# A spectral filter and a gated feed-forward on one core: weight columns in two loads, table points in parts, four more zero matmuls, and a tie of GpSimd copies to a scaling

## The chip, the core and the metric

The kernel runs on one core of a Trainium2 chip. Its instructions are issued by five engines: PE (TensorE, matmuls; PEld is its load of stationary operands), ACT (ScalarE), DVE (VectorE), POOL (GpSimd) and SP (SyncE, which here only issues DMAs; POOL issues DMAs too). The metric is the time of one execution on the device in microseconds, as the median of several runs. "0.3%" means 0.3% of that median.

## The reference

The input x has 2048 rows (S) of 576 numbers (D). A layer norm, a global filter in the frequency domain, a residual; then a second layer norm, a gated feed-forward of width 4608 and a second residual. All arrays are bf16.

```python
def _A_ref(x, w_r, w_i):                      # w_r, w_i: 2048 x 289
    X = jnp.fft.rfft2(x.astype(jnp.float32), axes=(-2, -1))
    X = X * (w_r + 1j * w_i)
    return jnp.fft.irfft2(X, s=(S, D), axes=(-2, -1)).astype(jnp.bfloat16)

def _B_ref(x, w_gate, w_up, w_down):
    return (_gelu(x @ w_gate) * (x @ w_up)) @ w_down

h = x + _A_ref(_layernorm(x), A_w_r, A_w_i)
h2 = h + _B_ref(_layernorm(h), B_w_gate, B_w_up, B_w_down)
```

## The kernel before

**How the work is laid out.** Row s = 16 p + c stands in partition p and tile c, so XO holds 16 tiles of 128 x 576. The transform over S is made as a 128-point step (over the partitions) and a 16-point step (over the tiles), the one over D as a product with cosine and sine tables. All of it is matmuls with tables that the kernel loads from DRAM.

**The order is written out by hand** in three strings of tokens, one token for each step, and `LOADS` hangs weight loads on tokens. Each engine executes its own instructions in the order in which they are emitted; `Prog` (`op`, `dma`, `emit`) turns the read and write keys of each operation into semaphore waits. Between two operations on PE no wait is made, except where the code asks for one (`after`); a DMA counts as done when its semaphore has its full count.

- `SEQ1` is the front. `B`/`b`/`S`/`Q` gather the statistics of a tile, `v`, `q`, `c` make the reciprocal deviation of a group of tiles (GROUPS: 2, 2, 3, 3, 3, 3 tiles), `x` (`ln1_scale`, L517) scales the 128-point table ATB into ATS with it, on DVE (`x0D`, `x1D`, `x5D`) or POOL (`x2P`, `x3P`, `x4P`), `n` and `t` copy parts of x on POOL, `M` (`a_mm`, L540) is the 128-point step of a group, `E`/`F` (`a_ev`) evacuate its banks into U. `k` (`idle_mm`, L533) issues matmuls of a zero tile into the bank that the next `M` uses first: `k14`, `k104`, `k202` are 14, 4 and 2 of them, for groups 0, 1 and 2.
- `SEQF` is the middle, 16 groups g of frequencies in the order `GORD` (1 to 15, then 0, which is group number 15 in the string). `D`/`d` (`st_D`, L630, matmuls at L640) is the product with FT over D and its evacuation CUS; `B` (`st_B`, L654) is the 16-point step with the table BT; `T` (`st_T`, L665, on DVE at L673) multiplies by the spectral weights WS; `V`/`v` (`st_V`, L675) and `R`/`r` (`st_R`, L690) are the inverse 16-point step with the table VT, the first for 256 columns, the second for the remaining 32 of four groups at once; `r` moves its result into VR with small DMAs on SP and POOL. BT and VT have one part for groups 1 to 15 and others for group 0 (g = 0, the last one done); for `R` there is a reordered copy of each.
- `SEQ` is the end of the filter: `I`/`i` (`i_mm`, L822; matmuls at L830, which read V and, in the last of three steps, VR) and `N`/`o` (L840) are the inverse steps over D and S, `a` (`x_add`) adds the residual, `s`, `q`, `c`, `n` make the second norm, `u`/`U` (`turn_mm`) transpose a tile and `e` (`turn_ev`) evacuates it into HT0. `G0` and `G1` (`gu_first`, L954) are gate and up products of the first two feed-forward blocks (m = 0 and 1), for the first 256 rows and the next 256.

After that comes the feed-forward over four blocks of 512 rows: for each of 36 blocks f of 128 columns `gu_part` (L924, matmuls at L939), Gelu on ACT (L947), the product on DVE (L948), and then `down_pass` (L1039). In the first block, the second half of the filter's rows is done in between (`deferred`).

**Loads.** `LORD` gives the order of x and ATB on SP; behind it come, in this order on SP: FT, BT, the first half of the spectral weights (`w_up`, `w_down` for both planes), VT, the second half, the zero group (`w_zero`). `dup_w` then makes the duplicates of WS in the other 64 partitions: for the first groups two copies by POOL (L730) and two by DVE (L728), for the others DMAs issued by POOL, which wait for the weights. `last` is the last of these DMAs; `tab_load` (at `r0`) makes SP wait for it and then loads DT, IT and IDT. `tab2_load` (at `.i7`) loads DP and ITD.

**The first feed-forward weights** (slot 0: 576 rows of gate and of up, columns 0 to 1152, blocks f = 0 to 8) are loaded in ten DMAs by `wg0_part`, each behind a `hold()`: SP waits until PE has finished everything emitted for it so far. Only the tenth writes the keys of the slot, and all ten count on one semaphore, so that every matmul of f = 0 to 8 waits for all ten. Slots 1 and 2 follow behind G0, where SP and POOL both hold.

**Where things lie.** HT0 shares its place with FT, BT and VT, so HT0 waits until these have been read.

Of the kernel before, what the change touches and what calls it, by code (L numbers as in the profile page):

```python
# [15 lines left out]
NT = 16  # L16
# [6 lines left out]
GROUPS = ((0, 2), (2, 4), (4, 7), (7, 10), (10, 13), (13, 16))  # L23
SEQ1 = """B0 b0 S3 B2 Q3 n0 B1 b1 b2 n1 t0 m3P t2 v0 v1 n2 t1 q0 c0 k14 x0D q1 M0 E0A S4 m4P c1 x1D n3 E2A k104 b5 t3 b7 Q4 E1A M1 E7A B5 B6 E8A b6 B7 v2 q2 B11 E5A B8 c2 x2P E3A E9A b8 b9 B9 v3 E6A n4 B12 Q13 E4A k202 M2 b10 q3 c3 b11 S13 x3P E11A B10 t4 b12 v4 E10A B14 m13P E14A M3 q4 c4 x4P E12A E13A t5 b14 E15A b15 B15 v5 E16A E18D E17A q5 M4 E20A E19A E23A c5 x5D n5 E24A F24D F23D E21A M5 E25A E26D E22A E28D E27A E29D F25A F29D F26A F27A F28A F22A""".split()
LORD = "x0-2 x2-4 a0-4 x4-8 a4-8 x8-12 x12-16 a8-16".split()
# [4 lines left out]
DENG, BENG = ['act', 'dve', 'act', 'act', 'act', 'act', 'act', 'act', 'dve', 'act', 'act', 'act', 'act', 'act', 'act', 'act'], ['act', 'dve', 'act', 'act', 'act', 'act', 'act', 'dve', 'act', 'act', 'act', 'act', 'act', 'act', 'act', 'act']  # L30
LOADS = {"r0": "t", "v12": "0", "v15": "1", ".I0": "2", ".i1": "3", ".N0": "4", ".i3": "5", ".o1": "6", ".N3": "7", ".o3": "8 9", ".i7": "d"}
RENG = ['dve', 'act', 'act', 'act', 'act']
# [14 lines left out]
def build_tables():  # L47
# [106 lines left out]
    assert np.allclose(VN[0, 0], VN[0, 1])  # L154
    T["VTAB"] = np.stack([VN[0, 0], VN[1, 0], VN[1, 1]] + [v.reshape(128, 4, 16, 4).transpose(0, 1, 3, 2).reshape(128, 256) for v in (VN[0, 0], VN[1, 0], VN[1, 1])], 1).reshape(128, -1)

# [175 lines left out]
def _build(nc, A_x, A_w_r, A_w_i, B_w_gate, B_w_up, B_w_down, out):  # L332
# [90 lines left out]
    def bank(b, p0=0, p1=128, c0=0, c1=512):  # L423
        return PS[p0:p1, b * 512 + c0:b * 512 + c1]
# [21 lines left out]
    P.dma(SP, FT[:, :, :].rearrange("p a b -> p (a b)"), dram["FTAB"][:, :], "ft", w=["FT"])  # L446
    P.dma(SP, BT[:, :, :, :].rearrange("p a b c -> p (a b c)"), dram["BTAB"][:, :], "bt", w=["BT"])

# [20 lines left out]
    for pl in (1, 0):  # L469
        w_up(pl, 0)  # L470
        w_down(pl, 0)
    P.dma(SP, VT[:, :, :, :].rearrange("p a b c -> p (a b c)"), dram["VTAB"][:, :], "vt", w=["VT"])
    for pl in (1, 0):
        w_up(pl, 1)
        w_down(pl, 1, (0, 1, 2, 3) if pl else (0, 1))
    for pl in (1, 0):
        w_zero(pl)
    GORD = list(range(1, NG)) + [0]
    wkeys = [[("W", hf, pl, h) for pl in range(2) for h in range(6 if hf < 2 else 2)] for hf in range(3)]
# [175 lines left out]
    def st_B(i, eng=ACT):  # L655
        sl, s3, sp_ = i % NY, i % 3, 1 if GORD[i] == 0 else 0
        b0 = FB["B", i]
        for m in range(2):
            for h in range(2):
                P.op(PE, lambda t, m=m, h=h: t.matmul(bank(b0 + h, 0, 128, 0, KW), BT[64 * h:64 * h + 64, sp_, m, :], CUS[64 * h:64 * h + 64, s3, m, :], start=(m == 0), stop=(m == 1)),  # L660
                     r=[("CU", s3), "BT"], w=[("PS", b0 + h)])
        ev(eng, YS[:, sl, :, :], banks(b0, 2, KW), [("PS", b0), ("PS", b0 + 1)], [("Y", sl)])
# [13 lines left out]
    def st_V(i, second, engs):  # L676
        g, z, b0 = GORD[i], i % NZ, FB["V", i]

        def mm(h, o, ct, first, last, after):
            c, t_ = ct  # L680
            return P.op(PE, lambda t: t.matmul(bank(b0 + o, 0, 128, 128 * c, 128 * c + 128), TP[64 * h:64 * h + 64, z, o, t_, c:256:2], VT[64 * h:64 * h + 64, 0 if g else 1 + o, t_, :],  # L681
                                               start=first, stop=last), r=[("T", z), "VT"], w=[("PS", b0 + o)], after=after)

        halves(("V", i), second, [[(c, t_) for c in range(2) for t_ in range(2)]] * 2, mm)
        if not second:
            return
        v5 = V[:, :, :, :, g, :, :].rearrange("p c t n j e -> p j (c t n) e")
        n = 2 // len(engs)
        for a, e in enumerate(engs):
            ev(e, v5[:, n * a:n * a + n], banks(b0 + a, n, 256).rearrange("p a (c e) -> p a c e", e=4), [("PS", b0 + a + k) for k in range(n)], [("V", g, a + k) for k in range(n)])  # L690

    def st_R(q, second):
# [3 lines left out]
        def mm(h, o, pt, first, last, after):  # L696
            part, t_ = pt
            return P.op(PE, lambda t: t.matmul(bank(b0 + o, 0, 128, 128 * part, 128 * part + 128), TR[64 * h:64 * h + 64, q % 2, o, t_, :], VT[64 * h:64 * h + 64, 4 + o if part else 3, t_, :], start=first, stop=last),  # L698
                        r=[("TR", q % 2, j) for j in range(4)] + ["VT"], w=[("PS", b0 + o)], after=after)

# [18 lines left out]
    def dup_w(k, jp, pl=slice(0, 2), eng=None):  # L719
        a, b = 64 * jp, 64 - 64 * jp  # L720
        n = ("Wd", k, jp, pl.start)
        for g0, g1 in (((1, 6),), ((6, 9),), ((9, 13),), ((13, 16), (0, 1)))[k]:
            dst, src = (WS[q:q + 64, jp, pl, g0:g1, :].rearrange("p a g k -> p a (g k)")[:, :, 1:] for q in (b, a))
            r = [x for x in (wkeys[1] if g0 > 8 else wkeys[0] if g0 else wkeys[0] + wkeys[2]) if pl.start <= x[2] < pl.stop]
            if eng is None:
                op = P.dma(POOL, dst, src, f"wd{k}{jp}", r=r, w=[(*n, g0)])
            elif eng == DVE:
                P.op(DVE, lambda v: v.tensor_copy(dst, src), r=r, w=[(*n, g0)])  # L728
            else:
                P.op(POOL, lambda v: v.tensor_scalar(dst, src, 1.0, 1.0, op0=ALU.mult, op1=ALU.mult), r=r, w=[(*n, g0)])  # L730
        return op if eng is None else None
# [32 lines left out]

    def wg0_part(k):
        hold()
        src = (B_w_gate, B_w_up)[k % 2]
        if k < 8:
            P.dma(SP, WG3[:, 0, 4 * (k % 2) + k // 2, :], src[(0, 128, 320, 448)[k // 2]:(128, 256, 448, 576)[k // 2], 0:1152], "wg00")
        else:  # L770
            P.dma(SP, WG3[64 * (k % 2):64 * (k % 2) + 64, 0, 8, :], src[256:320, 0:1152], "wg00", w=[("WG", 0, i) for i in range(4)] if k == 9 else [])

    def loads(w):
        for v in LOADS.get(w, "").split():
            (tab_load if v == "t" else tab2_load if v == "d" else lambda: wg0_part(int(v)))()

# [18 lines left out]
    P.alias(sum(wkeys, []) + sum(dup, []), [("WG", j, k) for j in (1, 2) for k in range(4)])  # L795
    P.alias(["FT", "BT", "VT"], [("HT", 0, i, k) for i in range(4) for k in range(5)])

# [128 lines left out]
    def gu_part(m, second, c0=0, c1=512):  # L926
# [5 lines left out]
        for j in range(n):  # L932
            for half in range(2):
# [6 lines left out]
                    bank(b, 0, 128, c0, c1), wg_tile(slot)[h0:h0 + 64, wt, 128 * (f % 9):128 * (f % 9) + 128], HT[h0:h0 + 64, kt, c0:c1], start=s, stop=e),  # L940
                    r=[("HT", tb % 2, i, k) for i in range(c0 // 128, c1 // 128) for k in range(5)] + [("WG", slot, i) for i in range(4)],
                    w=[("PS", b)], after=aft)
# [182 lines left out]
```

## Time and profile before

| what | value |
|---|---|
| time, median of 3 runs (lowest to highest) | 488.34 us (487.86 to 489.21) |
| the profiled execution | 487.7 us, span 485.9 us |
| PE busy, 23.84 to 43.67 us | 19.77 of 19.83 us |
| PE busy, 43.67 to 57.22 us | 11.55 of 13.55 us |
| gate/up matmuls (L939), us busy | 233.3 with WG, 53.4 with WGX |
| down matmuls (L1039), us busy | 132.9 |
| the ten loads of slot 0, from issue to landing | 3.2 to 5.0 us, median 3.8 |
| DMA engines, 44 to 56 us | 3.16 MB, 263 GB/s |

A profile is one execution, seen by the hardware profiler. Its span runs from the first to the last instruction; the time around it is longer. "Busy" is the time in which an engine works; rows of instructions give start, duration, engine, source line, operation, output and inputs, shape and count, and in square brackets the idle time just before and what ended it. Pieces of the chain of waits give start, duration and what. Rows of loads give target, source, issuing queue, count, size of each and the median of the microseconds from issue to landing. "SPq" and "POOLq" are issues of DMAs; the share of the DMA engines is the mean busy share of 16 engines and can show a little over 1.

### The profile page before, as it was taken

How to read it: one execution, taken by the hardware profiler on the slowest of the kernel's cores; microseconds unless marked ns; L12 is line 12 of the kernel's file. 1: busy time of each engine (PE TensorE's matmuls, PEld its weight loads, DVE VectorE, ACT ScalarE, POOL GpSimd, SP SyncE). 2: the span in 40 equal slices, each digit the busy share in tenths (PEclk: the TensorE clock that was granted, in tenths of full speed). 3: DMA queues.
4: the chain of work that ended last, by engine and by line, in shares of the span. 5: the costliest groups of instructions: out<-in, count | busy, mean ns of one | idle time of the engine just before them, and what ended most of it. 6: DMA issues, size and time to landing. Idle time of an engine off the chain costs nothing.

```text
span 485.9 us, 12883 instructions
## 1 busy us (share of the span) xinstructions
PE 476.7 (98%) x5872; PEld 279.4 (57%) x5872; DVE 182.9 (38%) x366; ACT 146.6 (30%) x295; POOL 52.8 (11%) x88
## 2 busy tenths in 40 slices
PE   7899899999999999999999999999999999999998
PEld 3777665544477744444577644444777444444774
DVE  7898756566501133333200233333101233333011
ACT  6998664443400023322200023322100133223000
POOL 6873317010120000000000000000000000000000
PEclk9999999999999999999999999999999999999999
DMA  8965598941440001100000011000000000000000
GB/s 287 210 161 177 175 306 285 377 110 24 131 143 26 27 15 20 23 0 1 1 15 15 26 21 23 14 2 1 3 13 26 14 1 0 1 1 1 3 26 26
DMA packets 26966, 33.19 MB, mean 68 GB/s; under 512 B 12560, under 2 KB 19104, under 8 KB 26912
## 3 DMA queue, kind: packets, MB, share of 16 engines
q1 hardware_dynamic: 23248, 19.87, 14.7%
q0 software_dynamic: 3664, 12.50, 8.0%
q8 instruction: 46, 0.75, 0.7%
q14 instruction: 8, 0.07, 0.0%
HBM read 26.21 MB, written 2.36 MB: 59 GB/s over the span
## 4 chain that ended last, share of the span: by engine, by line
PE 93%; DMA 1%; DVE 0%; issue 0%; SPq 0%; DVEq 0%
PE PS L939 58%; PE PS L1039 27%; PE PS L1051 2%; PE PS L640 2%; PE PS L681 2%; DMA WG<-in_B_w_up_dram 1%; PE PS L830 1%; PE PS L660 1%; PE PS L989 1%; PE PS L847 1%; PE PS L1006 0%; PE PS L698 0%; DVE CUS L606 0%; DVE V L606 0%; SPq L242 0%
## 5 line engine op out<-in xcount | busy, mean ns | idle before, releaser
L939 PE MATMUL PS<-HT,WG 64*128 64x512 bf16 (+1 forms) x2142 | 233.3, 372 | 1.2 <-DMA WG<-in_B_w_up_dram 1.2
L939 PEld LDWEIGHTS PS<-HT,WG 64*128 64x128 bf16 x2142 | 105.2, 94 | 116.1 <-DMA WG<-in_B_w_up_dram 1.3
L947 ACT ACTIVATE GL<-PS 128x512 bf16<-128x512 f32 x144 | 85.7, 596 | 282.9 <-PE PS L939 282.9
L948 DVE TENSOR_TENSOR AT<-GL,PS 128x512 bf16<-128x512 bf16 x144 | 98.8, 687 | 167.1 <-ACT GL L947 167.1
L1039 PE MATMUL PS<-WD,AT 64*128 64x288 bf16 x2160 | 132.9, 283 | 0.0
L1039 PEld LDWEIGHTS PS<-WD,AT 64*128 64x128 bf16 x2160 | 103.3, 94 | 29.8
L1026 DVE TENSOR_TENSOR OS<-PS,XO 128x288 bf16<-128x288 f32 (+2 forms) x32 | 13.3, 453 | 125.5 <-PE PS L1039 118.0
L939 PE MATMUL PS<-HT,WGX 64*128 64x512 bf16 x486 | 53.4, 376 | 0.0
L939 PEld LDWEIGHTS PS<-HT,WGX 64*128 64x128 bf16 x486 | 23.2, 94 | 29.2
L856 ACT ACTIVATE OS<-XO,NM 128x576 bf16<-128x576 bf16 x15 | 11.6, 774 | 11.4 <-DVE XO L1010 11.4
L640 PE MATMUL PS<-FT,U 64*128 64x288 bf16 x160 | 13.5, 284 | 0.3 <-DVE CUS L606 0.3
L673 DVE TENSOR_TENSOR TP<-YS,WS 128x1024 bf16<-128x1024 bf16 x16 | 11.0, 688 | 0.5 <-DMA WS<-WS 0.5
L551 PE MATMUL PS<-ATS,XO 128*128 128x128 bf16 x96 | 8.2, 219 | 3.0 <-POOL ATS L520 2.1
L494 DVE BATCH_NORM_STATS2 ST<-XO 128x6 f32<-128x288 bf16 x26 | 9.9, 441 | 2.1 <-DMA XO<-in_A_x_dram 2.0
L562 ACT ACTIVATE U<-PS 128x384 bf16<-128x384 f32 (+2 forms) x31 | 10.4, 419 | 1.1 <-PE PS L551 0.9
L681 PE MATMUL PS<-VT,TP 64*128 64x128 bf16 x256 | 10.0, 217 | 0.0
L242 POOL DMA_DIRECT2D WG<-in_B_w_gate_dram x9 | 6.1, 678 | 35.1 <-DMA WG<-in_B_w_gate_dram 30.6
L551 PEld LDWEIGHTS PS<-ATS,XO 128*128 128x128 bf16 x96 | 6.9, 98 | 4.4 <-POOL ATS L520 2.9
L242 POOL DMA_DIRECT2D WD<-in_B_w_down_dram x9 | 6.7, 755 | 24.4 <-PE PS L1006 24.4
L606 ACT ACTIVATE CUS<-PS 128x576 bf16<-128x576 f32 x14 | 9.0, 653 | 0.8 <-PE PS L640 0.7
L1051 PE MATMUL PS<-WD,AT 128*128 128x448 bf16 (+1 forms) x72 | 9.0, 286 | 0.0
L606 ACT ACTIVATE YS<-PS 128x576 bf16<-128x576 f32 x14 | 8.8, 653 | 0.2
(88 smaller groups left out, 229.5 us busy)
## 6 DMA issues: line engine op xcount, KB each, us to landing
WD<-in_B_w_down_dram POOLq DMA_DIRECT2D x9, 576.0 KB, 10.6
WG<-in_B_w_up_dram SPq DMA_DIRECT2D x6, 576.0 KB, 6.8
WG<-in_B_w_gate_dram POOLq DMA_DIRECT2D x6, 576.0 KB, 5.8
out_dram<-OS SPq DMA_DIRECT2D x30, 72.0 KB, 1.7
XO<-in_A_x_dram SPq DMA_DIRECT2D x3, 576.0 KB, 7.5
WG<-in_B_w_gate_dram SPq DMA_DIRECT2D x4, 288.0 KB, 3.8
WG<-in_B_w_up_dram SPq DMA_DIRECT2D x4, 288.0 KB, 3.6
WGX<-in_B_w_up_dram SPq DMA_DIRECT2D x2, 576.0 KB, 4.6
```

The source lines that it names most:

```text
L242: fn = lambda e: e.dma_start(out_ap, in_ap)
L551: P.op(PE, lambda t, b=b, lhs=lhs, p0=p0, p1=p1, s=s, e=e, o=o, c=c: t.matmul(bank(b, p0, p1, o, o + 128), lhs, ATS[:, c, :], start=s, sto ...
L606: fn = (lambda v: v.tensor_copy(dst, src)) if eng == DVE else (lambda a: a.activation(dst, src, ACTF.Copy))
L640: return P.op(PE, lambda t: t.matmul(bank(b0 + o, 0, 128, 0, 2 * HK), U[64 * h:64 * h + 64, us, 2 * i:2 * i + 2, :, :], FT[64 * h:64 * h + ...
L681: return P.op(PE, lambda t: t.matmul(bank(b0 + o, 0, 128, 128 * c, 128 * c + 128), TP[64 * h:64 * h + 64, z, o, t_, c:256:2], VT[64 * h:64 ...
L856: P.op(ACT, lambda a, c=c, out=out: a.activation(out, XO[:, c, 0:D], ACTF.Square, bias=NM[:, c:c + 1], accum_out=SB2[:, 1, c:c + 1]), r=[( ...
L939: op = P.op(PE, lambda t, h0=h0, kt=kt, wt=wt, b=b, s=(not second and j == 0), e=(second and j == n - 1): t.matmul(bank(b, 0, 128, c0, c1) ...
L947: P.op(ACT, lambda a: a.activation(GL[:, s2, :], bank(b0), ACTF.Gelu_apprx_tanh), r=[("PS", b0)], w=[("GL", s2)])
L948: P.op(DVE, lambda v: v.tensor_tensor(AT[:, f, :], GL[:, s2, :], bank(b0 + 1), op=ALU.mult), r=[("GL", s2), ("PS", b0 + 1)], w=[("AT", f)])
L1026: P.op(DVE, lambda v: v.tensor_tensor(OS[:, p % 2, d0:d1], bank(b, 0, 128, 0, d1 - d0), XO[:, c, d0:d1], op=ALU.add), r=[("PS", b), ("X", ...
L1039: e[h] = P.op(PE, lambda t, f=f, h=h, r0=r0, j=j: t.matmul(bank(b0 + h, 0, 128, 0, 288), AT[r0:r0 + 64, f, 128 * p:128 * p + 128], WD[r0:r ...
L1051: P.op(PE, lambda t, b=b, d0=d0, d1=d1, f=f, j=j: t.matmul(bank(b, 0, 128, 0, d1 - d0), AT[:, f, 128 * p:128 * p + 128], WD[:, f, d0:d1], ...
```

## The change

- In `SEQ1`, `k202` becomes `k206`: six zero matmuls before the 128-point step of group 2 instead of two.
- BT and VT are loaded in parts. BT: groups 1 to 15 (64 KB) at its old place, group 0 (64 KB, key BT1) after the zero group of the weights. VT: the table of `V` for groups 1 to 15 (64 KB) at its old place, that of `R` (64 KB, key VT1) after the zero group, those of group 0 (256 KB, key VT2) at the head of `tab_load`. The order inside VTAB changes to suit.
- The POOL copies in `dup_w` also read the key of the last tile of ATS, and so wait for `x5D` on DVE.
- Slot 0 is loaded by columns: six DMAs of columns 0 to 256 (f = 0 and 1) at `.I0`, which count on a semaphore of their own and write the key WGA, and six of columns 256 to 1152 at `.N0`, `.i3`, `.o1`, `.N3` and `.o3`. A load takes 256 rows (two tiles) or 64 rows. Blocks m = 0 and 1 wait for WGA alone. At `v12`, `v15` and `.i1` nothing is loaded any more.

```diff
...
-... c2 x2P E3A E9A b8 b9 B9 v3 E6A n4 B12 Q13 E4A k202 M2 b10 ...
+... c2 x2P E3A E9A b8 b9 B9 v3 E6A n4 B12 Q13 E4A k206 M2 b10 ...
...
-LOADS = {"r0": "t", "v12": "0", "v15": "1", ".I0": "2", ".i1": "3", ".N0": "4", ".i3": "5", ".o1": "6", ".N3": "7", ".o3": "8 9", ".i7": "d"}
+LOADS = {"r0": "t", ".I0": "a0 a1 a2 a3 a4 a5", ".N0": "b0", ".i3": "b1", ".o1": "b2", ".N3": "b3", ".o3": "b4 b5", ".i7": "d"}
...
     assert np.allclose(VN[0, 0], VN[0, 1])
-    T["VTAB"] = np.stack([VN[0, 0], VN[1, 0], VN[1, 1]] + [v.reshape(128, 4, 16, 4).transpose(0, 1, 3, 2).reshape(128, 256) for v in (VN[0, 0], VN[1, 0], VN[1, 1])], 1).reshape(128, -1)
+    T["VTAB"] = np.stack([v if k else v.reshape(128, 4, 16, 4).transpose(0, 1, 3, 2).reshape(128, 256) for v, k in ((VN[0, 0], 1), (VN[0, 0], 0), (VN[1, 0], 1), (VN[1, 1], 1), (VN[1, 0], 0), (VN[1, 1], 0))], 1).reshape(128, -1)
...
     P.dma(SP, FT[:, :, :].rearrange("p a b -> p (a b)"), dram["FTAB"][:, :], "ft", w=["FT"])
-    P.dma(SP, BT[:, :, :, :].rearrange("p a b c -> p (a b c)"), dram["BTAB"][:, :], "bt", w=["BT"])
+    P.dma(SP, BT[:, 0, :, :].rearrange("p b c -> p (b c)"), dram["BTAB"][:, 0:256], "bt", w=["BT"])
...
         w_down(pl, 0)
-    P.dma(SP, VT[:, :, :, :].rearrange("p a b c -> p (a b c)"), dram["VTAB"][:, :], "vt", w=["VT"])
+    P.dma(SP, VT[:, 0, :, :].rearrange("p b c -> p (b c)"), dram["VTAB"][:, 0:256], "vt", w=["VT"])
...
         w_zero(pl)
+    P.dma(SP, VT[:, 1, :, :].rearrange("p b c -> p (b c)"), dram["VTAB"][:, 256:512], "vt1", w=["VT1"])
+    P.dma(SP, BT[:, 1, :, :].rearrange("p b c -> p (b c)"), dram["BTAB"][:, 256:512], "bt1", w=["BT1"])
...
                 P.op(PE, lambda t, m=m, h=h: t.matmul(bank(b0 + h, 0, 128, 0, KW), BT[64 * h:64 * h + 64, sp_, m, :], CUS[64 * h:64 * h + 64, s3, m, :], start=(m == 0), stop=(m == 1)),
-                     r=[("CU", s3), "BT"], w=[("PS", b0 + h)])
+                     r=[("CU", s3), "BT1" if sp_ else "BT"], w=[("PS", b0 + h)])
...
             c, t_ = ct
-            return P.op(PE, lambda t: t.matmul(bank(b0 + o, 0, 128, 128 * c, 128 * c + 128), TP[64 * h:64 * h + 64, z, o, t_, c:256:2], VT[64 * h:64 * h + 64, 0 if g else 1 + o, t_, :],
-                                               start=first, stop=last), r=[("T", z), "VT"], w=[("PS", b0 + o)], after=after)
+            return P.op(PE, lambda t: t.matmul(bank(b0 + o, 0, 128, 128 * c, 128 * c + 128), TP[64 * h:64 * h + 64, z, o, t_, c:256:2], VT[64 * h:64 * h + 64, 0 if g else 2 + o, t_, :],
+                                               start=first, stop=last), r=[("T", z), "VT" if g else "VT2"], w=[("PS", b0 + o)], after=after)
...
             part, t_ = pt
-            return P.op(PE, lambda t: t.matmul(bank(b0 + o, 0, 128, 128 * part, 128 * part + 128), TR[64 * h:64 * h + 64, q % 2, o, t_, :], VT[64 * h:64 * h + 64, 4 + o if part else 3, t_, :], start=first, stop=last),
-                        r=[("TR", q % 2, j) for j in range(4)] + ["VT"], w=[("PS", b0 + o)], after=after)
+            return P.op(PE, lambda t: t.matmul(bank(b0 + o, 0, 128, 128 * part, 128 * part + 128), TR[64 * h:64 * h + 64, q % 2, o, t_, :], VT[64 * h:64 * h + 64, 4 + o if part else 1, t_, :], start=first, stop=last),
+                        r=[("TR", q % 2, j) for j in range(4)] + ["VT2" if part else "VT1"], w=[("PS", b0 + o)], after=after)
...
             else:
-                P.op(POOL, lambda v: v.tensor_scalar(dst, src, 1.0, 1.0, op0=ALU.mult, op1=ALU.mult), r=r, w=[(*n, g0)])
+                P.op(POOL, lambda v: v.tensor_scalar(dst, src, 1.0, 1.0, op0=ALU.mult, op1=ALU.mult), r=r + [("ATS", NT - 1)], w=[(*n, g0)])
...
         P.op(SP, None, after=[last])
+        P.dma(SP, VT[:, 2:6, :, :].rearrange("p a b c -> p (a b c)"), dram["VTAB"][:, 512:1536], "vt2", w=["VT2"])
...
 
-    def wg0_part(k):
+    def wg0_part(k, f0, f1, keys):
         hold()
-        src = (B_w_gate, B_w_up)[k % 2]
-        if k < 8:
-            P.dma(SP, WG3[:, 0, 4 * (k % 2) + k // 2, :], src[(0, 128, 320, 448)[k // 2]:(128, 256, 448, 576)[k // 2], 0:1152], "wg00")
+        o, src = k % 2, (B_w_gate, B_w_up)[k % 2]
+        if k < 4:
+            r0 = 320 * (k // 2)
+            P.dma(SP, WG3[:, 0, 4 * o + k // 2 * 2:4 * o + k // 2 * 2 + 2, f0:f1], src[r0:r0 + 256, f0:f1].rearrange("(t p) f -> p t f", p=128), f"wg0{f0}")
         else:
-            P.dma(SP, WG3[64 * (k % 2):64 * (k % 2) + 64, 0, 8, :], src[256:320, 0:1152], "wg00", w=[("WG", 0, i) for i in range(4)] if k == 9 else [])
+            P.dma(SP, WG3[64 * o:64 * o + 64, 0, 8, f0:f1], src[256:320, f0:f1], f"wg0{f0}", w=keys if k == 5 else [])
...
         for v in LOADS.get(w, "").split():
-            (tab_load if v == "t" else tab2_load if v == "d" else lambda: wg0_part(int(v)))()
+            if v in "td":
+                (tab_load if v == "t" else tab2_load)()
+            else:
+                wg0_part(int(v[1]), *((0, 256, ["WGA"]) if v[0] == "a" else (256, 1152, [("WG", 0, i) for i in range(4)])))
...
     P.alias(sum(wkeys, []) + sum(dup, []), [("WG", j, k) for j in (1, 2) for k in range(4)])
-    P.alias(["FT", "BT", "VT"], [("HT", 0, i, k) for i in range(4) for k in range(5)])
+    P.alias(["FT", "BT", "VT", "BT1", "VT1", "VT2"], [("HT", 0, i, k) for i in range(4) for k in range(5)])
...
                     bank(b, 0, 128, c0, c1), wg_tile(slot)[h0:h0 + 64, wt, 128 * (f % 9):128 * (f % 9) + 128], HT[h0:h0 + 64, kt, c0:c1], start=s, stop=e),
-                    r=[("HT", tb % 2, i, k) for i in range(c0 // 128, c1 // 128) for k in range(5)] + [("WG", slot, i) for i in range(4)],
+                    r=[("HT", tb % 2, i, k) for i in range(c0 // 128, c1 // 128) for k in range(5)] + (["WGA"] if m < 2 else [("WG", slot, i) for i in range(4)]),
...
```

More of the change, by code (lines that the diff above doesn't have):

```diff
@@ L23 @@
 GROUPS = ((0, 2), (2, 4), (4, 7), (7, 10), (10, 13), (13, 16))
-SEQ1 = """B0 b0 S3 B2 Q3 n0 B1 b1 b2 n1 t0 m3P t2 v0 v1 n2 t1 q0 c0 k14 x0D q1 M0 E0A S4 m4P c1 x1D n3 E2A k104 b5 t3 b7 Q4 E1A M1 E7A B5 B6 E8A b6 B7 v2 q2 B11 E5A B8 c2 x2P E3A E9A b8 b9 B9 v3 E6A n4 B12 Q13 E4A k202 M2 b10 q3 c3 b11 S13 x3P E11A B10 t4 b12 v4 E10A B14 m13P E14A M3 q4 c4 x4P E12A E13A t5 b14 E15A b15 B15 v5 E16A E18D E17A q5 M4 E20A E19A E23A c5 x5D n5 E24A F24D F23D E21A M5 E25A E26D E22A E28D E27A E29D F25A F29D F26A F27A F28A F22A""".split()
+SEQ1 = """B0 b0 S3 B2 Q3 n0 B1 b1 b2 n1 t0 m3P t2 v0 v1 n2 t1 q0 c0 k14 x0D q1 M0 E0A S4 m4P c1 x1D n3 E2A k104 b5 t3 b7 Q4 E1A M1 E7A B5 B6 E8A b6 B7 v2 q2 B11 E5A B8 c2 x2P E3A E9A b8 b9 B9 v3 E6A n4 B12 Q13 E4A k206 M2 b10 q3 c3 b11 S13 x3P E11A B10 t4 b12 v4 E10A B14 m13P E14A M3 q4 c4 x4P E12A E13A t5 b14 E15A b15 B15 v5 E16A E18D E17A q5 M4 E20A E19A E23A c5 x5D n5 E24A F24D F23D E21A M5 E25A E26D E22A E28D E27A E29D F25A F29D F26A F27A F28A F22A""".split()
 LORD = "x0-2 x2-4 a0-4 x4-8 a4-8 x8-12 x12-16 a8-16".split()
```

## The prediction

> **What bounds the kernel now.** I read the page first, then the chain of waits, then the timelines of the engines around the two places the change touches, and last the loads.
>
> From the page:
>
> ```profile
> span 485.9 us, 12883 instructions
> ...
> PE 476.7 (98%) x5872; PEld 279.4 (57%) x5872; DVE 182.9 (38%) x366; ACT 146.6 (30%) x295; POOL 52.8 (11%) x88
> ...
> PEclk9999999999999999999999999999999999999999
> ```
>
> TensorE is busy for all but 9.2 us of the span and at full granted clock throughout, and the change takes no matmul away. So only idle time of PE, or of whatever feeds it, can be won. The chain of waits (start, duration, what) shows the one large piece that is not PE:
>
> ```profile
> 51.78 0.39 SPq L242
> 52.17 0.04 issue
> 52.22 4.96 DMA WG<-in_B_w_up_dram
> 57.17 0.05 issue
> 57.22 6.32 PE PS L939 x92
> ```
>
> The tenth load of slot 0 is issued at 52.22, lands at 57.17, and releases the first gate/up matmul. The timelines of PE, ACT and DVE say what PE did meanwhile:
>
> ```profile
> 55.84 0.22 PE L899 MATMUL PS<-IDT,HN 64*128 64x64 bf16 x4
> 57.22 6.33 PE L939 MATMUL PS<-HT,WG 64*128 64x256 bf16 x92 [1.16 <-DMA WG<-in_B_w_up_dram]
> 54.64 1.38 ACT L606 ACTIVATE HT<-PS 128x640 bf16<-128x640 f32 x2
> 56.72 0.81 DVE L606 CAST HT<-PS 128x640 bf16<-128x640 f32 x1
> ```
>
> PE ends its transposes at 56.06, and ACT has written HT tiles 1 and 0 by 56.02: without the weights G0 would be free at about 56.08. G0 and G1 together last 3.9 us (57.22 to the first 512-column matmul at 61.1). The banks do not hold it: the slots as the code hands them out give G0 the banks of u2 (evacuated on DVE by 55.89) and u0 (the ACT copy that ends 56.02), while N5, which DVE still reads until 56.80, has banks 6 and 7.
>
> In front, the timelines of PE, POOL and DVE:
>
> ```profile
> 12.92 0.23 PE L551 MATMUL PS<-ATS,XO 128*128 128x128 bf16 x1 [2.06 <-POOL ATS L520]
> 18.67 2.86 POOL L730 TENSOR_SCALAR WS<-WS 64x1444 bf16<-64x1444 bf16 x2 [0.61 <-DMA WS<-in_A_w_i_dram]
> 17.81 0.62 DVE L525 TENSOR_SCALAR ATS<-ATB,RS 128x128 bf16<-128x128 bf16 x3
> 22.04 1.07 DVE L728 COPY WS<-WS 64x1444 bf16<-64x1444 bf16 x2 [0.89 <-DMA WS<-in_A_w_r_dram]
> 23.84 0.42 PE L640 MATMUL PS<-FT,U 64*128 64x288 bf16 x4 [0.30 <-DVE CUS L606]
> 28.66 0.70 DVE L673 TENSOR_TENSOR TP<-YS,WS 128x1024 bf16<-128x1024 bf16 x1 [0.47 <-DMA WS<-WS]
> ```
>
> M2 waits 2.06 us for a POOL scaling; at 22.04 the DVE copies wait for spectral weights, the evacuation of D1 stands behind them, and PE loses 0.30 us to it; T5 waits 0.47 us for a duplicated weight. From 23.84 to 43.67 PE shows 19.77 us busy of 19.83 and DVE 18.99: two engines full, PE a little fuller.
>
> **The change, part by part.** The sum is made against the profiled execution: 487.7 us, of it 485.9 span and 1.8 around it. It lies 0.64 below the median of 488.34, and I carry the difference over unchanged.
>
> *Slot 0 in two column parts.* Ten SP loads become six of columns 0:256 behind I0 and six of columns 256:1152 behind N0, i3, o1, N3 and o3. The total is the same 2.65 MB, but v12 and v15 issue nothing any more, so the first load starts at 44.97 (today's third) instead of 43.43. SP's issues cost 0.33 to 0.60 us each: six end by about 47.4. Today's ten loads land 3.2 to 5.0 us after issue, so WGA is there by 52.4, with 3.7 us to spare before 56.08. The first four groups of G0 and G1 read only this part, so the 1.16 us wait goes: **-1.14**. Late next is f=2, which needs columns 256:1152 at 56.08 + 3.9 = 60.0. Its last two loads keep the position of today's last two (51.65, 52.22). If the backlog there is unchanged they land at 57.2. At worst the 1.54 us later start comes on top, and 590 KB in 512-byte rows at the 208 GB/s of the stretch 14 to 15 us (load of the 16 engines 1.08 there) instead of 313, which is 0.95 us: 59.7. The 313 is 3.13 MB (weights plus DP and ITD) by the 10.0 us that the busy shares of 44 to 57 us add up to. Both ends lie under 60.0: cost 0, cover 0.3 to 2.8 us. SP's DP and ITD keep their place behind i7; their user runs at 63.3. Behind G0 the holds of SP and POOL release slot 1 as much earlier as G0 ends.
>
> *BT in two parts.* 64 KB less ahead of the first spectral weights. These rows carry it:
>
> ```profile
> VT<-c_vtab SPq DMA_DIRECT2D x1, 384.0 KB, 9.7
> ...
> BT<-c_btab SPq DMA_DIRECT2D x1, 128.0 KB, 10.4
> ...
> WS<-in_A_w_r_dram SPq DMA_DIRECT2D x2, 126.4 KB, 4.7
> ```
>
> A 128 KB table that takes 10.4 us to land stands in a queue. The bytes saved are worth 64 KB at 410 GB/s (10 to 11 us) = 0.16 us, up to 64 KB at 204 = 0.32; if descriptors rather than bytes count (still 128) it is 0. PE can gain at most its 0.30 us at 23.54. I take **-0.2**, between 0 and -0.30.
>
> *VT in three parts.* 384 KB before the second weight half become 64 KB, and VT1 and BT1 (64 KB each) come after the zero-group rows: 256 KB net leave the queue until 27 us, 0.6 to 1.25 us by the same two rates. The second-half weights and the GpSimd-issued duplicates then land earlier, and T5's 0.47 us on DVE goes. PE gets only that part which today reaches it as gaps too short for a row of their own: 0 to -0.47, I take **-0.15**. VT1 has a new place in the queue, SP's last before the VR copies. The last zero-row load is issued at 23.64 and takes 5.3 us; VT1 follows at about 24.2. The share of the DMA engines falls to 0.21 at 27 to 28 us; less 256 KB it drains about 0.8 us earlier, and VT1 lands between 26.5 and 28.9. R0 needs it at 28.87 minus the gain ahead: cost 0, at worst 0.5. BT1 is read by group 15 alone, after 40 us. VT2 (256 KB) goes ahead of DT, IT and IDT: one more SP issue of 0.45 us behind the wait for the last duplicate (37.55, likely 0.2 to 0.8 earlier now). DT lands at worst at 40.6 + 0.85 + 0.45 = 41.9 and is used at 44.5; IT at 43.5, used at 46.7; VT2 itself by 41, used by V15 at 43. Behind them on SP stand the VR copies of r1 and r2: the last is issued at 41.99 and lands 3.2 us later, at 45.2, with i0 needing it at 45.74. Half a microsecond of cover against at most 0.45: cost 0, at worst 0.4.
>
> *Four more zero matmuls.* The present two start at 10.26 and take 0.59; PE then stands until 12.92. Fourteen of them took 4.91 us, 0.35 each at most: four more end by 12.3. Cost 0, cover 0.6. Gain 0: the matmuls behind the 2.06 us gap follow every 55 ns, as elsewhere.
>
> *The tie.* The copies at 18.67 wait now also for x5D, over at 18.43. Behind them on POOL are the duplicates' issues at 22.31, which wait for w_r anyway. Cost 0; if the weights came much earlier, POOL would lose what they win, but not DVE.
>
> Sum: -1.14 - 0.2 - 0.15 = -1.5, so 487.7 - 1.5 = 486.2 for a profiled execution, and **486.8** for the median.
>
> **Rivals.** (A) The forecast, with the front part between -0.1 and -0.6: 486.6 to 487.1. Chance 0.50, of it 0.37 on the faster side of 0.3% (1.47 us, at 486.87 - about what a measurement can tell), since its middle lies just past that line and a leaner queue helps at several short gaps.
>
> (B) The front gives nothing or takes back: VT1 late at R0 or VR late at i0 (0.4 to 0.5), against the DMA wait of 1.14 gained. 487.2 to 487.7. For it: R0's thin margin. Against: 256 KB fewer ahead. Chance 0.19, all within 0.3%.
>
> (C) The front gives more: the 0.30 of PE, all of T5's 0.47 and some 0.3 of the short gaps, on top of 1.14: 488.34 - 2.2 = 486.1. For it: DVE and PE are both full there, and both are released. Against: PE shows 0.06 us idle in that stretch. Chance 0.13.
>
> (D) The second column part is late and f=2 waits. Its bytes must end 1.1 us before landing (today 56.1 and 57.2). Counting from 46.2, when the flow starts, 3.13 MB must run at 3.13 / 12.7 us = 246 GB/s to cost nothing, and below 227 the kernel is slower than before. At the 185 GB/s of the stretch 12 to 13 us (share 1.07, short rows) the bytes end at 63.1, f=2 starts at 64.2 in place of 61.1, and with 0.35 from the front it is 488.34 + 2.75 = 491.1. For it: 512-byte rows and a later start. Against: four fifths of the bytes still go in rows of 1792 bytes, near today's 2304. Chance 0.13, slower. The Trainium skill, DMA: Bandwidth & Descriptors, section Bandwidth, speaks for this one: it asks for transfers of 1 MiB or more and shows 138 GB/s for 64 KB against 341 for 1 MB. An estimate by that page, 590 KB of 32 and 128 KB loads at 138, adds 2.4 us instead of 0.95, and f=2 would wait about 1.1 us, leaving 487.9. The trace agrees with it only in part: 288 KB loads, several in flight, reach 313.
>
> (E) PE does not start earlier, as something else ends at 57.2: 488.0 to 488.3. The rows above show all of G0's inputs done by 56.1. Chance 0.05.
>
> **How the numbers follow.** Faster: 0.37 of A and C = 0.50. Same: 0.13 of A, B but for 0.01, E = 0.36. Slower: D and 0.01 of B = 0.14. The range goes from C less half a microsecond of spread between runs (487.86 to 489.21 today) to 488.6, past B and E and the mild part of D: 485.7 to 488.6.
>
> **What would show it.** Right: the first L939 matmuls start near 55.7 with no DMA as releaser, the DVE copies of the spectral weights a little before 22.04, no wait at f=2. Wrong: a wait of L939's first 512-column matmuls on WG (D), a wait of L698 on VT or of L830 on VR (B), M2 later than 12.92 (zeros), or POOL's copies starting well after 18.67 (tie).

## The result, and the profile after

The changed kernel takes 486.22 us (median of 20 executions, 485.72 to 488.05); the kernel before, on the same chip beside it, 487.62 us (20 executions, 486.54 to 489.21). The ratio is 0.9973 [0.9963, 0.9982], so the change takes off 1.40 us. The predicted difference was 1.5. The predicted 486.8 stands above 486.22 because it was counted down from the median of three runs, 488.34, and 20 runs gave 487.62; from there the same difference leads to 486.1.

The profiled execution took 485.97 us, with a span of 484.2 us (before 487.7 and 485.9). The page of the changed kernel:

```profile
span 484.2 us, 12895 instructions
...
PE 477.5 (99%) x5875; PEld 304.4 (63%) x5876; DVE 183.3 (38%) x366; ACT 146.3 (30%) x295; POOL 52.2 (11%) x88
```

TensorE's busy time grew by 0.8 us (about what the additional zero matmuls take) and the span shrank by 1.7: about 2.5 us of idle time are gone, of which the zeros only fill 0.8. The chain of waits at the place where the tenth load stood (start, duration, what):

```profile
55.02 0.34 PE PS L854 x4
55.36 0.06 PE PS L906 x4
55.42 0.06 issue
55.47 6.31 PE PS L946 x92
```

No DMA is left in it: PE goes from the transposes (L906) straight into gate and up (L946, the old L939). The timelines of PE, ACT, DVE and POOL, at the places shown of before:

```profile
12.54 0.23 PE L553 MATMUL PS<-ATS,XO 128*128 128x128 bf16 x1 [0.84 <-POOL ATS L522]
18.18 2.86 POOL L732 TENSOR_SCALAR WS<-WS 64x1444 bf16<-64x1444 bf16 x2 [0.51 <-DVE ATS L527]
17.43 0.62 DVE L527 TENSOR_SCALAR ATS<-ATB,RS 128x128 bf16<-128x128 bf16 x3
20.80 1.35 DVE L730 COPY WS<-WS 64x1444 bf16<-64x1444 bf16 x2
22.62 0.78 PE L642 MATMUL PS<-FT,U 64*128 64x288 bf16 x10
27.57 0.70 DVE L675 TENSOR_TENSOR TP<-YS,WS 128x1024 bf16<-128x1024 bf16 x1 [0.23 <-PE PS L683]
45.10 0.34 PE L837 MATMUL PS<-DT,VR 64*128 64x288 bf16 x2 [0.33 <-issue]
53.99 1.38 ACT L608 ACTIVATE HT<-PS 128x640 bf16<-128x640 f32 x2
```

Four waits of before are gone or smaller: PE stands 0.84 us ahead of M2 instead of 2.06 (the zeros fill most of the difference; M2 itself starts 0.38 us earlier), the DVE copies of the spectral weights wait for no DMA, the products D5 and D3 run through in one row of ten where PE stood 0.30 us, T5 no longer waits for a duplicated weight. One wait is new: the first matmul on VR, 0.33 us instead of 0.06. The POOL copies start when DVE's last scaling has ended: the tie is what releases them.

The same milestones in both traces, in us from the start of the span, and what each stretch gave:

| milestone | before | after | gained since the row above |
|---|---|---|---|
| first matmul of D2 | 20.30 | 19.91 | 0.39 |
| first matmul of D3 | 23.84 | 22.99 | 0.46 |
| first matmul of I0 | 44.52 | 43.62 | 0.05 |
| first matmul on VR | 45.74 | 45.10 | -0.26 |
| first matmul of G0 | 57.22 | 55.47 | 1.11 |
| end of the span | 485.9 | 484.2 | about 0 |

The loads of slot 0: the six of the first column part are issued from 44.07 to 46.63 and have landed by 49.84, with G0 ready at 55.42. The six of the second part are issued from 47.27 to 52.14, the last lands at 58.59, and f=2 starts at 59.40 without a wait: 0.8 us of cover.

### The profile page after: what moved, and what is told of

It reads as the page before. It is cut to its first block, busy times and chain, and to the rows that moved or that the text cites. A ratio compares the mean times of both kernels' runs of the same rounds, so it can differ in the third digit from the quotient of the medians.

```text
span 484.2 us, 12895 instructions
## 1 busy us (share of the span) xinstructions
PE 477.5 (99%) x5875; PEld 304.4 (63%) x5876; DVE 183.3 (38%) x366; ACT 146.3 (30%) x295; POOL 52.2 (11%) x88
## 4 chain that ended last, share of the span: by engine, by line
PE 95%; DMA 1%; DVE 1%; POOL 1%; SPq 0%; issue 0%; POOLq 0%; DVEq 0%
PE PS L946 58%; PE PS L1046 27%; PE PS L642 2%; PE PS L1058 2%; PE PS L683 2%; DMA XO<-in_A_x_dram 1%; PE PS L553 1%; PE PS L662 1%; PE PS L837 1%; PE PS L996 1%; DVE XO L860 1%; SPq L242 0%; PE PS L1013 0%; PE PS L854 0%; POOL XN L569 0%
## 5 line engine op out<-in xcount | busy, mean ns | idle before, releaser
L946 PE MATMUL PS<-HT,WG 64*128 64x512 bf16 (+1 forms) x2142 | 233.5, 373 | 0.1
L946 PEld LDWEIGHTS PS<-HT,WG 64*128 64x128 bf16 x2142 | 116.1, 94 | 104.4 <-DVE AT L955 0.2
L1046 PEld LDWEIGHTS PS<-WD,AT 64*128 64x128 bf16 x2160 | 114.3, 94 | 18.7
L946 PE MATMUL PS<-HT,WGX 64*128 64x512 bf16 x486 | 53.5, 376 | 0.0
L946 PEld LDWEIGHTS PS<-HT,WGX 64*128 64x128 bf16 x486 | 25.7, 94 | 26.7
L538 PE MATMUL PS<-ZD 128*128 128x512 bf16 x23 | 7.5, 484 | 1.5 <-POOL ZD L431 1.5
```

Of the source, the lines that this page charges most:

```text
L946: op = P.op(PE, lambda t, h0=h0, kt=kt, wt=wt, b=b, s=(not second and j == 0), e=(second and j == n - 1): t.matmul(bank(b, 0, 128, c0, c1) ...
L1046: e[h] = P.op(PE, lambda t, f=f, h=h, r0=r0, j=j: t.matmul(bank(b0 + h, 0, 128, 0, 288), AT[r0:r0 + 64, f, 128 * p:128 * p + 128], WD[r0:r ...
```

## The experiments

**My theory** was that the columns win the wait at G0, the parted tables some tenths in front, and that the zeros and the tie do nothing. **The rivals** were that the tables give nothing or take back what they give at VR, and that zeros or tie, costed at nothing, carry a part of the gain. Each execution also has its span and its mean granted TensorE clock on record. Line numbers differ a little from kernel to kernel.

### One part of the change alone

`e1_columns` is the kernel before with the two column parts of slot 0 and nothing else:

```diff
-LOADS = {"r0": "t", "v12": "0", "v15": "1", ".I0": "2", ".i1": "3", ...
+LOADS = {"r0": "t", ".I0": "a0 a1 a2 a3 a4 a5", ".N0": "b0", ".i3": "b1", ...
```

> The kernel before with slot 0 loaded by columns and nothing else of the change. Theory (parts add up): the 1.16 us wait of the first L939 matmul on WG goes and nothing else moves, so -1.1 us (-0.23%), and the time from the first VR matmul of L830 to the first L939 matmul is 10.4 us instead of 11.5. Rival (the change's gain comes from the front): less than -0.5 us. The front up to 44 us should stand where it stands in the kernel before, give or take what one run differs from another.

487.16 us (12 executions) against 487.77 (29): ratio 0.9987 [0.9974, 1.0]. From the timeline of PE:

```profile
46.40 0.34 PE L834 MATMUL PS<-DT,VR 64*128 64x288 bf16 x2 [0.37 <-issue]
56.77 5.60 PE L943 MATMUL PS<-HT,WG 64*128 64x256 bf16 x85
```

From the first matmul on VR to G0 it is 10.37 us, 1.11 less than the 11.48 of before: the columns give what was expected of them, in the stretch where it was expected. The whole time gained only 0.6, about half of what was expected, with an interval that just reaches no change. Two things in this one profile run against it: 0.37 us of wait at VR (0.06 before), and 0.71 us at D3, where this kernel still has the old order of loads.

`e2_tables` has only the parts of BT and VT:

```diff
-    ... BT[:, :, :, :] ... dram["BTAB"][:, :], "bt", w=["BT"])
+    ... BT[:, 0, :, :] ... dram["BTAB"][:, 0:256], "bt", w=["BT"])
...
-    ... VT[:, :, :, :] ... dram["VTAB"][:, :], "vt", w=["VT"])
+    ... VT[:, 0, :, :] ... dram["VTAB"][:, 0:256], "vt", w=["VT"])
...
+    ... "vt1", w=["VT1"])
+    ... "bt1", w=["BT1"])
...
+    ... "vt2", w=["VT2"])
```

> The kernel before with BT and VT loaded in parts and nothing else: no columns, no tie, two zero matmuls. Theory: the spectral weights land earlier, D3 is not held by the DVE copies (-0.4 us), the VR copies of r2 become the last thing the first VR matmul waits for (+0.3), and the wait on WG stays: -0.2 to -0.6 us in all. Rival (the earlier front of the changed kernel was the luck of one execution): 0.0, with the DVE copies starting at 21.5 to 22.1 us as before.

487.39 us (12) against 487.77; ratio 0.9998 [0.9981, 1.0016]: not told apart from no change. The timelines of DVE and PE:

```profile
21.15 1.08 DVE L730 COPY WS<-WS 64x1444 bf16<-64x1444 bf16 x2
22.97 0.77 PE L642 MATMUL PS<-FT,U 64*128 64x288 bf16 x10
45.53 0.35 PE L833 MATMUL PS<-DT,VR 64*128 64x288 bf16 x2 [0.41 <-DMA VR<-RB]
56.48 5.83 PE L942 MATMUL PS<-HT,WG 64*128 64x256 bf16 x87 [0.64 <-DMA WG<-in_B_w_up_dram]
```

In front it does what the change does: the copies no longer wait, ten matmuls of D5 and D3 in one row. Behind that stand 0.41 us at VR and 0.64 at G0: what is won ahead of a wait for loads seems to be partly swallowed there. A wait at G0 stays as long as slot 0 is loaded in whole rows.

`e3_tie_zeros` has only the six zero matmuls and the tie:

```diff
-... Q13 E4A k202 M2 b10 ...
+... Q13 E4A k206 M2 b10 ...
...
-... r=r, w=[(*n, g0)])
+... r=r + [("ATS", NT - 1)], w=[(*n, g0)])
```

> The kernel before with the tie and the six zero matmuls and nothing else. Theory: 0.0 (within 0.3 us), POOL copies at 18.5 to 18.8 us. Rival (the tie or the zeros carry a part of the gain): more than 0.4 us either way, with the first matmul after the zeros moved.

487.84 us (12) against 487.77; ratio 0.9995 [0.9978, 1.0011]: no difference, as expected. The timeline of PE has a wait of 1.06 us ahead of M2, and at VR and G0:

```profile
46.42 0.34 PE L830 MATMUL PS<-DT,VR 64*128 64x288 bf16 x2 [0.41 <-DMA VR<-RB]
57.85 4.32 PE L939 MATMUL PS<-HT,WG 64*128 64x256 bf16 x74 [1.10 <-DMA WG<-in_B_w_up_dram]
```

VR is late here although VT is whole: VT2 ahead of DT isn't needed for that.

`e4_before_again` is the kernel before without an edit, for a second profile.

> The kernel before once more, for one profile. It tells how much of the 0.38 us by which the third x load (10.53 before, 10.14 after the change) and the first matmul of group 2 stand earlier is the difference between two executions: theory, all of it, so here the load lands between 10.0 and 10.7 and the copies of the weights (22.04) move with it. Rival: 10.5 again, and 22.0 again, and then the change itself moved them.

488.87 us, span 487.1, and a mean granted clock of 0.996, where the first profile of the same kernel had 1.000. The timeline shows the wait ahead of M2, the windows of 1 us from there show the clock (columns: window, its length, busy time of PE, PEld, DVE, ACT and POOL, granted clock, load of the DMA engines, GB/s):

```profile
12.98 0.23 PE L551 MATMUL PS<-ATS,XO 128*128 128x128 bf16 x1 [2.03 <-POOL ATS L520]
```

```profile
12.00:13.00 1.00, 0.02 (x1) 0.03 (x2) 1.00 (x6) 0.94 (x4) 0.83 (x1) 1.00 1.04 282
13.00:14.00 1.00, 1.00 (x17) 1.00 (x18) 1.00 (x5) 1.00 (x5) 0.83 (x1) 0.88 1.16 207
14.00:15.00 1.00, 1.00 (x12) 1.00 (x11) 1.00 (x6) 0.74 (x2) 0.83 (x1) 0.50 1.15 226
15.00:16.00 1.00, 1.00 (x12) 1.00 (x10) 0.22 (x1) 0.29 (x1) 0.62 (x2) 0.50 1.00 237
16.00:17.00 1.00, 1.00 (x12) 1.00 (x11) 0.58 (x3) 1.00 (x4) 0.32 (x1) 0.50 1.16 236
17.00:18.00 1.00, 1.00 (x19) 1.00 (x18) 1.00 (x6) 1.00 (x4) 0.87 (x2) 0.91 1.11 264
```

After 2.03 us without a matmul, PE runs at half clock from about 13.8 to 17.2 us (0.24 us of the second window, three whole ones, 0.18 of the last: 3.4 us), with 12 matmuls in a microsecond. From the first matmul of M2 to the first of M5 it is 6.66 us where the first profile had 5.61, and the first matmul of D2 stands at 22.08 instead of 20.30. With that shift DVE's last scaling meets the POOL copies:

```profile
18.73 1.74 DVE L525 TENSOR_SCALAR ATS<-ATB,RS 128x128 bf16<-128x128 bf16 x3
19.02 2.87 POOL L730 TENSOR_SCALAR WS<-WS 64x1444 bf16<-64x1444 bf16 x2 [0.16 <-POOL XN L567]
20.52 0.23 PE L551 MATMUL PS<-ATS,XO 128*128 128x128 bf16 x1 [0.50 <-DVE ATS L525]
```

Three scalings take 1.74 us instead of 0.62; the third alone takes 1.41, behind a POOL copy of 1.39 us that began 0.03 us before it, and M5 waits 0.50 us for it. In e1, and likewise in e2 and e9, the order is the other way round:

```profile
17.60 0.61 DVE L525 TENSOR_SCALAR ATS<-ATB,RS 128x128 bf16<-128x128 bf16 x3
18.00 2.94 POOL L730 TENSOR_SCALAR WS<-WS 64x1444 bf16<-64x1444 bf16 x2 [0.15 <-POOL XN L567]
```

There the third scaling began 0.03 to 0.04 us before the copy and took 0.24 us, and the copy took 1.46 to 1.47 instead of 1.39. A shift of less than a tenth of a microsecond decides which of the two is held. The Trainium skill, TensorE: Matmul & The Clock Gate, Part 1, knows the half clock, a window of about 3.4 us, and says the window runs freely, so that it is by chance where in it a gap falls; the half clock and its length agree with these windows, though the page asks for an idle window of about 3.4 us and here 2.03 us were enough, 1.75 in e10. The third scaling agrees with the Trainium skill, SBUF — State Buffer, section SBUF: two separate sides: of DVE and GpSimd, who comes first can hold the pair of ports they share for a whole instruction. That it is these ports is not shown here.

The question put to this run, whether the earlier start of the changed kernel is only the difference of two executions, stays open: the load of x tiles 8 to 11 landed at 10.58 here (10.53 before, 10.14 in the changed kernel), and the copies of the weights were shifted by the clock.

This gave a new rival to "cost 0, gain 0": zeros and tie guard against something that the profile before did not show.

### One part of the change undone

`e5_after_again` is the changed kernel without an edit.

> The changed kernel once more, beside the next three on the same chip. Theory: as measured, about 1.3 us under the kernel before; executions in one cluster, since the gap in front of the 128-point step of group 2 is only 0.8 us and POOL's copies cannot meet the scaling of group 5.

486.44 us (8) against 488.24 (30); ratio 0.9955 [0.9938, 0.9972]. Its wait at VR is 1.02 us:

```profile
45.93 0.34 PE L837 MATMUL PS<-DT,VR 64*128 64x288 bf16 x2 [1.02 <-DMA VR<-RB]
56.30 6.03 PE L946 MATMUL PS<-HT,WG 64*128 64x256 bf16 x89
```

Still no wait at G0 and none at f=2. The same kernel showed 0.33 us at VR above: this wait is a matter of the execution. R0, too, waits here, for the part of VT that was moved behind the zero group:

```profile
28.21 0.28 PE L700 MATMUL PS<-VT,TR 64*128 64x128 bf16 x4 [0.18 <-DMA VT<-c_vtab]
```

VT1 landed at 28.16, so both waits of rival B exist in the changed kernel.

`e6_no_tie` takes the tie out of the changed kernel, `e7_no_zeros` takes out the four zeros, `e9_columns_tables` both:

```diff
-... r=r + [("ATS", NT - 1)], w=[(*n, g0)])
+... r=r, w=[(*n, g0)])
```

```diff
-... Q13 E4A k206 M2 b10 ...
+... Q13 E4A k202 M2 b10 ...
```

> The changed kernel without the tie. The repeat of the kernel before showed a scaling of group 5 on DVE that took 1.41 us instead of 0.24, started 0.03 us after a POOL copy of 1.39 us. Theory (POOL's copy blocks the DVE scaling until it is done): with the weights landing at 16.7 the copies start near 17.7, one scaling takes 1.2 to 1.5 us, the matmuls of group 5 start 0.7 to 1.2 us later than 18.1, and the time is 0.4 to 1.0 us over the changed kernel in most executions. Rival (the tie is worth nothing, as predicted): within 0.3 us, scalings of 0.24 to 0.30.

> The changed kernel with two zero matmuls before group 2 instead of six. The repeat of the kernel before showed the granted clock at 0.5 from about 13.9 to 17.2 us, after 2.03 us in which PE stood still. Theory (the longer gap lets the clock fall in a part of the executions): a second cluster of executions 0.8 to 1.4 us above the first, median 0 to 1.0 us over the changed kernel; if the profiled execution is of the second cluster it shows a clock under 1 between 13 and 18 us. Rival (zeros worth nothing, as predicted): one cluster, within 0.3 us of the changed kernel.

> The changed kernel without the tie and without the four zero matmuls: columns and table parts alone. Theory: both effects of the two runs before it, so 0.5 to 1.5 us over the changed kernel, near the kernel before less 0.2 to 0.8. Rival: as fast as the changed kernel.

Against 488.24 us (30): without the tie 486.22 (11), ratio 0.9959 [0.9944, 0.9974]; without the zeros 487.08 (12), ratio 0.9974 [0.996, 0.9989]; without both 486.45 (12), ratio 0.9971 [0.9954, 0.9988]. The losses that were expected came in one of the three: e7 stands 0.64 us over the changed kernel (486.44 beside it) with two groups of executions. Without the tie nothing is lost, where 0.4 to 1.0 us was expected, but in its profile DVE had begun well before POOL, so that the meeting of e4 was not tried:

```profile
18.12 2.87 POOL L732 TENSOR_SCALAR WS<-WS 64x1444 bf16<-64x1444 bf16 x2 [0.32 <-DMA WS<-in_A_w_i_dram]
17.53 0.62 DVE L527 TENSOR_SCALAR ATS<-ATB,RS 128x128 bf16<-128x128 bf16 x3
```

Without the zeros the wait ahead of M2 is back, and at VR stands 0.24:

```profile
12.81 0.23 PE L553 MATMUL PS<-ATS,XO 128*128 128x128 bf16 x1 [1.85 <-POOL ATS L522]
45.75 0.35 PE L837 MATMUL PS<-DT,VR 64*128 64x288 bf16 x2 [0.24 <-issue]
```

Sorting the executions of the experiments by their mean granted clock settles what the zeros do. 3.4 us at half clock make 0.9965 of 486 us, and the executions have either 1.000 or 0.996 to 0.997 (one each of e2 and e3, which took over a millisecond, are left out here):

| zeros ahead of M2 | kernels | executions below full clock |
|---|---|---|
| two | before, beside the experiments | 30 of 85 |
| two | e1, e2, e7, e9 | 3 of 12, 3 of 11, 5 of 12, 2 of 12 |
| two | e4, e10, e11 (one execution each) | 3 of 3 |
| six | changed kernel, e5, e6, e8, e12 | 0 of 20, 0 of 8, 0 of 11, 0 of 6, 0 of 10 |
| six | e3 | 1 of 11 |

With two zeros 46 of 135, with six 1 of 66. In the kernel before the lowered clock costs 1.5 us (median 489.12 of 30 against 487.64 of 55). It costs 0.9 us with the tie (e7: 487.55 of 5 against 486.65 of 7) and 2.1 without (e9: 488.41 of 2 against 486.27 of 10); so the tie would save about 1.2 us once the clock falls. That rests on seven slowed executions, and no profile shows the tie at work in one.

At full clock alone, each against the kernel before beside it: e1 486.93 (9), e2 487.25 (8) and e3 487.52 (10) against 487.50 (21); e9 486.27 (10), e7 486.65 (7), e6 486.22 (11) and e5 486.44 (8) against 487.78 (18). Tables and columns together (e9) give 1.5 us, all of what the whole change gives there (e5: 1.3); taking out zeros or tie moves it by 0.4 us at most, and two runs of the same kernel differ by 0.2. The columns alone give 0.6, the tables alone 0.25. That both together give more fits e2, where part of what the tables won ended in the wait at G0; it was not tested further.

### Where the wait at VR and the earlier weights come from

`e8_vt2_early` loads VT2 (256 KB) right behind BT1 instead of at the head of `tab_load`, where it stands ahead of DT and of the small copies that make VR; `e12_vt2_early_again` is the same kernel.

```diff
     ... "bt1", w=["BT1"])
+    ... "vt2", w=["VT2"])
...
     def tab_load():
         P.op(SP, None, after=[last])
-        ... "vt2", w=["VT2"])
```

> The changed kernel with VT2 (256 KB) loaded right behind BT1, in the stretch 26 to 29 us where the DMA engines are nearly idle, and not ahead of DT. Theory A (the 256 KB ahead of DT delay the VR copies of r2 and so the first VR matmul, 0.33 us in the changed kernel): the VR copies land at or before 44.4, the idle time before the first VR matmul falls under 0.1 us, -0.2 to -0.3 us. Theory B (the copies of r2 are late by their own chain: evacuation, five or three issues of 0.5 to 0.6 us, 2 to 3.5 us to land, and the kernels without VT2 wait there too): the idle time stays between 0.06 and 0.45 us and the time within 0.2 us of the changed kernel.

> The changed kernel with VT2 behind BT1 once more. Its first profile showed 0.06 us of idle time before the first VR matmul, where seven profiles with VT2 ahead of DT show 0.08 to 1.02 and five with VT in one piece 0.06 to 0.41. Theory A (VT2's place matters): under 0.1 us again, and 0.2 to 0.5 us under the changed kernel's medians of 486.22 and 486.44. Theory B (the spread is that of single executions): anywhere between 0.06 and 0.45 us, and 486.1 to 486.5.

485.99 us (6) against 488.27 (11), ratio 0.9951 [0.9933, 0.997]; again 486.23 (10) against 488.33 (15), ratio 0.9961 [0.9946, 0.9976]. Both wait 0.06 us at VR. From the timelines of PE, first and second kernel:

```profile
43.67 1.16 PE L837 MATMUL PS<-DT,V 64*128 64x288 bf16 x16 [0.38 <-DVE V L609]
...
55.26 6.33 PE L946 MATMUL PS<-HT,WG 64*128 64x256 bf16 x92
```

```profile
55.80 6.33 PE L946 MATMUL PS<-HT,WG 64*128 64x256 bf16 x92
```

Over all profiles the wait at VR is 0.08 to 1.02 us, mean 0.38, with VT2 ahead of DT (seven), 0.06 to 0.41, mean 0.20, with VT whole (five), and 0.06 twice with VT2 early. That points at VT2's place, as the first expectation had it, but the times do not tell this version apart from the changed kernel (486.22 and 486.44), and a wait of 0.41 occurs with VT whole too. It stays open.

`e10_bt_only` parts BT alone, `e11_vt_only` VT alone, both on the kernel before.

> The kernel before with BT alone in two parts and VT whole at its old place. The last of the first-half real weights landed at 21.5 to 22.2 us in four profiles with whole tables and at 19.8 to 20.9 in six with parts; BT is the only part that lies ahead of it. Theory A (the queue is first in, first out, so only BT's 64 KB count): the landing is 20.3 to 21.0 here as well. Theory B (VT, issued 0.65 us after that load, shares the DMA engines with it while it is still in flight): 21.4 to 22.2 here.

> The kernel before with VT alone in three parts and BT whole at its old place. Theory A (only what is ahead counts): the last of the first-half real weights lands at 21.4 to 22.2 us as before. Theory B (VT's 320 KB behind it compete with it): 20.3 to 21.0.

489.60 and 489.68 us. Both executions fell to the lowered clock (0.997 and 0.996), so their times say nothing of the tables; in both, a scaling on DVE took 1.42 and 1.41 us behind a POOL copy. The page of the first shows the dip in the second slice:

```profile
PEclk9899999999999999999999999999999999999999
```

The loads can still be read. The last load of the real weights of the first half takes, from issue to landing, 8.2 to 9.0 us in four profiles with whole tables, 6.7 to 7.7 in eight with both parted, 7.0 with BT parted and 7.5 with VT parted. So, by one profile each, either part, 64 KB less ahead or 320 KB less behind, shortens it, and the two do not add up. How the load behind it slows it was not settled.

## Why the prediction was right, point by point

- **What bounds the kernel:** right. PE works all but 6.7 us of the span, and what the two profiles differ by is idle time of PE. The lowered clock, which is lost time of a busy PE, was not thought of.
- **Columns, -1.14:** right in place and size. G0 starts at 55.47 with no DMA as releaser (the prediction said near 55.7), and the stretch to it became shorter by 1.11 in the changed kernel and in e1 alone. f=2 did not wait: the last load landed at 58.59, between the bounds 57.2 and 59.7 that were worked out from the rows of before. So rival D fell. By the Trainium skill (DMA: Bandwidth & Descriptors, section Bandwidth), as estimated in the prediction, f=2 would have waited 1.1 us; the trace does not bear that out with several loads in flight. The cover is thin: 0.8 us here, 0.4 to 1.4 over the eight profiles with columns. The first part has far more to spare than it needs, 49.84 against 55.47.
- **BT in parts, -0.2, at most -0.30:** right mechanism, mis-sized. From issue to landing the last of the weights took 6.7 us instead of 8.6, where 64 KB at the two rates were to save 0.16 to 0.32, and PE gained 0.46 in the profiles compared; whether the parts of BT or of VT did it is not shown, as e11 shortens the landing too. The 0.30 was the idle time in the bracket, which starts only when the modelled length of the last matmul has run out. By starts, two matmuls of D that follow each other 0.12 us apart elsewhere stood 0.59 apart (23.25, the last of a row of six from 23.00, and 23.84): 0.47 lost. From D2 to D3 it takes 3.08 us wherever nothing waits, 3.54 and 3.95 in before and e1, 3.07 in e3 (whole tables, no wait by chance) and 3.27 in e12: the term is 0 to 0.9 by execution.
- **VT in parts, -0.15 through T5:** the wait for the DMA went, the gain did not come: D3 to I0 takes 20.68 and 20.63 us. DVE's wait was covered. VT1 landed at 27.82, and R0 at 28.07 did not wait; in e5 it waited 0.18 us, between the cost of 0 and the worst case of 0.5 that the prediction gave.
- **The VR copies, 0, at worst +0.4:** the bound was the better guess. The changed kernel lost 0.26 there, and 1.02 was seen. The copies have landed by 44.64 and the matmul starts at 45.10; PE takes four semaphore instructions in between, 0.11 us apart. The half microsecond of cover that the prediction read in the kernel before (45.22 to 45.74) is the same four instructions: PE stood idle only 0.06 us there, but nothing was left. This is the mechanism of rival B, at a part of its price; it did not decide because 1.1 us stood against it.
- **Zeros, cost 0 and gain 0:** the cost was right; the gain is the step that failed. The prediction reasoned from a profile with full clock, and the matmuls behind the gap do follow every 55 ns there. In a third of the executions they follow at half speed for 3.4 us, for 1.5 us of time, and six zeros prevent nearly all of it. On a median this weighs some 0.5 us: the 85 executions of before have 488.16, the 55 at full clock 487.64. How much of it is in the 487.62 of the result is not known, as the clock of those 20 is not on record.
- **The tie, cost 0:** right. That it can gain was not seen: it makes POOL start behind DVE's last scaling, which POOL's copy held up in all three profiles in which the clock had fallen.
- **The first 0.39** (up to D2) belongs to none of these: at full clock, D2 starts between 20.08 and 20.30 in the five profiles with two zeros, between 19.69 and 20.45 in the six with six. It follows the load of x tiles 8 to 11, the fourth of five, which landed at 10.53 before and at 10.14 after: D2 starts 9.8 to 9.9 us behind that landing in all eleven. Whether the parted tables move this load is not settled: it landed at 10.32 to 10.68 in the five profiles with BT whole and at 9.91 to 10.97 in the nine with BT parted.

The sum of the terms was -1.5; what can be put down to the change in the two profiles is -1.11 - 0.46 - 0.05 + 0.26 = -1.36, and the medians differ by -1.40. The two profiled executions differ by 1.73, the 0.39 ahead of D2 included. The terms in front erred both ways and nearly cancelled, and the medians contain an unknown share of lowered clock: that the total came out within 0.1 us is in part luck.

## What to carry to other kernels

Split a load so that the first consumer waits only for its own columns, and check the second part against the time that the first buys: here a wait of 1.16 us at the first consumer went, and the second part kept 0.4 to 1.4 us of cover. Measure a stall of a pipelined engine from start to start of its instructions, since the idle time in a row leaves part of it out. And take the mean granted clock of every execution, not of one profile: here a gap of 2 us in a chain of matmuls halved the clock for 3.4 us in a third of the executions, which no single profile at full clock could show.

## What the hardware showed that was not expected

- With a gap of 1.75 to 2.06 us between matmuls (by the profiles) the granted clock fell in 46 of 135 executions, in the three profiled ones to 0.5 for 3.4 us; with a gap of 0.67 to 1.15 us it fell in 1 of 66.
- A DVE scaling of 0.25 us (median) took 1.41, 1.42 and 1.41 us in three profiles in which a GpSimd copy of 1.39 us had begun about 0.03 us before it, and 0.24 us in three in which it had begun 0.03 to 0.04 us ahead of the copy.
- The landing of a load seems to depend on what is put in the queue behind it as well as ahead: 8.2 to 9.0 us with both tables whole, 7.5 with only the load behind made smaller (one profile).
